# Attention units with scores in one run over four PSUM banks, values in one run, and the side tasks split and spread

## The chip, the cores and the metric

The program runs on one core of one Trainium2 chip. The metric is the device time of one execution in microseconds; the kernel before took 880.97 us (median of three runs, 880.14 to 883.23). The profiled execution, from which all rows below come, took 881.46 us.

## What is computed

Two stages. The first is sliding-window attention with a linear bias by head; its output, one row of 512 numbers for each of 4,608 tokens, goes into the second, a mixture of eight experts in which each token is sent to one expert only.

```python
scores = scale * np.matmul(q, k.transpose(0, 1, 3, 2))       # q, k, v: (8, 8, 576, 64), float32
mask = (rel >= 0) & (rel < 128)
scores = np.where(mask, scores + bias[None], -1000000000.0)  # bias = -slope(head) * distance
attn = softmax(scores); x = np.matmul(attn, v)               # -> (4608, 512)
expert_idx = np.argmax(x @ w_gate, axis=1)                   # 8 experts
h = np.maximum(x_sorted[lo:hi] @ w1[e], 0.0)                 # 512 -> 1024
y_sorted[lo:hi] = h @ w2[e]                                  # 1024 -> 512
out = gate_w[:, None] * y
```

## The kernel before, in words

**Units.** The attention stage is cut into `NU` = 32 units: one for each of 8 batches and of 4 pairs of heads (`b, hp = divmod(u, HP)`). Each unit has, for its two heads (`par` 0 and 1, which lie in the two halves of the partitions):

- `scores`: transposed scores for five blocks of keys (`BLK`: 256, 256, 256, 192 and 64 queries), 10 matrix products per head pair, each two instructions on TensorE. A head has 1,024 score columns, that is two PSUM banks of 512 (`s` = 0 and 1), so a unit needs four banks `sp`. ScalarE takes the exponential of each bank into `e`, VectorE multiplies by a table of exp(bias) and mask into `probs` (`fac` for half 0, `fac2` for half 1).
- `merge` (GpSimd): two additions that fold overlapping blocks of `probs` into `mg`, so that the sums of the softmax cost fewer columns.
- `values`: `probs` times `v` for two stretches of queries (`SEG`, `s` = 0: 256 and `s` = 1: 320), each into a PSUM bank `xp`, which ScalarE copies to `xT`.
- `totals`: products with a column of ones that add up the sums of `probs` and `mg` in a bank `sm`; after a batch's fourth unit it is copied to `sT`.

The work of one unit is recorded beside that of the unit before: in step `u` TensorE gets the scores of unit `u` and the values and totals of unit `u - 1`. Before the change the order in a step is scores half 0, values half 0, scores half 1, values half 1, totals.

**Tasks.** When a batch is complete, a list of tasks is queued (`tasks_of`), which turn it into rows for the experts: two of `logits_t` (products with the gate's weights into a bank `m`, ScalarE copies to `lT`), `gate` (transposes of `lT` and `sT` in banks `m`; VectorE divides, reduces, picks the expert with `pick`; ScalarE has one small exponential `gex` per tile of 128 tokens), `row` (four transposes of `xT` into a bank `m`, VectorE scales them into `xs`, GpSimd writes the token's number), `place` (two small products on what `pick` left in `pre`, VectorE makes `slots`), and `send` (GpSimd scatters a tile's rows to `x_rows` in DRAM by an indirect DMA, line 174). An even batch has 4 tiles, an odd one 5. From step 8 on, 3 or 4 tasks are taken from the list at the end of each step; what is left after the last unit runs in a row.

**Order and buffers.** `tc.manual_schedule()` keeps the order of the code on every engine, so an instruction that waits holds up what stands behind it on its engine. The eight PSUM banks are: three for `sp`, two for `xp`, two for `m`, one for `sm`. Tiles of a pool rotate: a new one waits until the tile that had its bank has been read. `ex` has two buffers of each of `e`, `probs` and `mg`.

**Loads.** SyncE issues, in the code's order, the loads of a batch's q, k and v one batch ahead (two buffers), and in steps 1 to 8 `clear_rows`, eight writes of 1,285 KB that clear `x_rows` in DRAM; the first `send` waits for the last of them.

After the attention come the experts (`gather` reads `x_rows` back; `layer1`, `layer2`), which the change does not touch. Lines from 504 on stand a few lines lower after the change.

Of the kernel before, what the change touches and what calls it, by code (L numbers as in the profile page):

```python
# [8 lines left out]
F32 = mybir.dt.float32  # L9
I32 = mybir.dt.int32  # L10
AX = mybir.AxisListType.X
AF = mybir.ActivationFunctionType
# [9 lines left out]
def kernel(  # L22
# [320 lines left out]
    with tc.tile_pool(name="tab", bufs=1) as tab, \  # L343
# [4 lines left out]
         tc.tile_pool(name="ps_s", bufs=3, space=PSUM) as ps_s, \  # L348
         tc.tile_pool(name="ps_x", bufs=2, space=PSUM) as ps_x, \
         tc.tile_pool(name="ps_1", bufs=1, space=PSUM) as ps_1, \  # L350
         tc.tile_pool(name="ps_m", bufs=2, space=PSUM) as ps_m:
# [37 lines left out]
        probs, xps, mgs, sums = {}, {}, {}, {}  # L389
# [16 lines left out]
        def scores(u, s):  # L406
            b, hp = divmod(u, HP)
            if s == 0:
                probs[u] = ex.tile([P, 2, W], F32, name="probs")
            blocks = [x for x in BLK if x[1] // (W // 2) == s]  # L410
            sps = [ps_s.tile([P, W // 2], F32, name="sp") for _ in range(2)]
            for j, c, q0, n in blocks:
                c -= s * (W // 2)
                for par in range(2):
                    half = slice(par * HALF, (par + 1) * HALF)
                    nc.tensor.matmul(  # L416
                        sps[par][:, c : c + n], lhsT=k_sb[b][half, hp, k_lo[j] : k_lo[j] + P],
                        rhs=q_sb[b][half, hp, q0 : q0 + n], start=True, stop=True,
                    )
            e = ex.tile([P, 2, W // 2], F32, name="e")  # L420
            for par in range(2):
                nc.scalar.activation(e[:, par, :], sps[par][:], AF.Exp, scale=D ** -0.5)  # L422
# [20 lines left out]
        def values(u, s):  # L443
# [5 lines left out]
            xp = ps_x.tile([P, S - 2 * P], F32, name="xp")  # L449
# [53 lines left out]
        def gate(ts):  # L503
            t0, n = ts[0], len(ts)
            tt = slice(t0, t0 + n)
            lgw = rows.tile([P, GT, H, E], F32, name="lgw", bufs=1)
            for i0 in range(0, n, 2):
                two = range(i0, min(i0 + 2, n))
                m = ps_m.tile([P, 2, 3 * HALF], F32, name="m")
                for i in two:  # L510
                    pair, c = ts[i] // TP, ts[i] % TP * P
                    nc.tensor.transpose(m[:, i - i0, :P], lT[pair][:, c : c + P], ident[:])
                    nc.tensor.transpose(m[:, i - i0, P:], sT[pair][:, c : c + P], ident[:64, :64])
                nc.vector.reciprocal(
                    rs_all[:, t0 + i0 : t0 + i0 + len(two), :].rearrange("p t (g a) -> p t g a", a=2),
                    m[:, : len(two), P:].rearrange("p t (a g) -> p t g a", a=2)[:, :, :HP, :],
                )
                for i in two:
                    nc.vector.tensor_tensor(
                        lgw[:, i].rearrange("p (g a) e -> p g a e", a=2),  # L520
                        m[:, i - i0, :P].rearrange("p (g r) -> p g r", r=32)[:, :, : 2 * E]
                        .rearrange("p g (a e) -> p g a e", a=2),
                        rs_all[:, ts[i], :].rearrange("p (g a) -> p g a", a=2).unsqueeze(3).to_broadcast([P, HP, 2, E]),
                        op=ALU.mult,
                    )
# [10 lines left out]
        xs_of = {}  # L536
# [24 lines left out]
        def tasks_of(b):  # L561
            t0 = b // 2 * TP + b % 2 * KT
            tiles = list(range(t0, t0 + KT + b % 2))
            ts = [lambda: logits_t(b, 0), lambda: logits_t(b, 1)]
            ts += [lambda: gate(tiles), lambda: row(tiles, 0), lambda: place(tiles, rows, ps_m, "m"), lambda: row(tiles, 1)]
            for i in range(2, len(tiles)):
                ts.append(lambda i=i: (send(tiles, i - 2), row(tiles, i)))
            return ts + [lambda i=i: send(tiles, i) for i in (len(tiles) - 2, len(tiles) - 1)]

        with tc.manual_schedule():  # L570
# [3 lines left out]
            tasks = []  # L574
            for u in range(NU + 1):
                b, hp = divmod(u, HP)
                if u < NU:
# [6 lines left out]
                    scores(u, 0)  # L584
                if u > 0:
                    values(u - 1, 0)
                if u < NU:
                    scores(u, 1)
                    merge(u)
                if u > 0:  # L590
# [263 lines left out]
```

## Time and profile before

| | us |
|---|---|
| median of 3 runs | 880.97 |
| profiled execution | 881.46 |
| its span, first to last instruction | 879.70 |
| start to the scores of unit 2 | 20.91 |
| units 2 to 7, no tasks | 29.43 |
| units 8 to 31, with tasks | 191.36 |
| last values, last batch's tasks, gather | 24.94 |
| experts | 613.06 |

The five stretches are cut where TensorE starts the scores of unit 2 and of unit 8, the values of unit 31, and the first transposes of the experts. A row of the timeline gives start, duration, engine, line, operation, tiles out<-in, and in brackets how long the engine was idle before it and what ended that. Neighbours of one group on one engine are merged (x8: eight instructions). TensorE's matmuls overlap, so that starts, not durations, tell how long a group holds the engine.

### The profile page before, as it was taken

The page shows a single profiled execution, that of the slowest core. Times are in us where ns is not written, and L with a number is a line of the kernel's source. Part 1 is how long each engine was busy: PE and PEld are TensorE (multiplying, and loading weights), DVE is VectorE, ACT ScalarE, POOL GpSimd, SP SyncE. Part 2 cuts the span into 40 slices and gives each one's busy share as a digit, 9 for nine tenths or more (in the row PEclk, how much of TensorE's full clock was granted, in tenths as well). Part 3 has the DMA queues.
Part 4 walks back from the last instruction along what each step waited for, and adds up shares of the span by engine and source line. Part 5 has one row for each costly group of instructions (what it writes and reads, how often), then busy time and mean ns, then how long its engine had stood idle before and what let it go on. Part 6 is the DMA issues. An engine that isn't in the chain of part 4 may idle for free.

```text
span 879.7 us, 10068 instructions
## 1 busy us (share of the span) xinstructions
PE 827.6 (94%) x4162; PEld 516.8 (59%) x4162; DVE 222.2 (25%) x475; ACT 176.4 (20%) x410; POOL 176.7 (20%) x189
## 2 busy tenths in 40 slices
PE   6998988999958999999999999999999999999993
PEld 4765666666636745754754664674575575475471
DVE  4556556656673100110110120120011011010010
ACT  3653443554410101010100101000100010101010
POOL 5645444566430001001001001001000100100100
PEclk9998898999968999999999999999999999999997
DMA  9997761561125203301600700600420240050060
GB/s 347 347 357 257 262 216 65 214 216 38 37 97 209 102 25 135 144 16 58 235 12 37 258 1 36 251 11 32 164 114 25 83 187 12 37 212 13 36 219 4
DMA packets 47334, 112.54 MB, mean 128 GB/s; under 512 B 3503, under 2 KB 3503, under 8 KB 47280
## 3 DMA queue, kind: packets, MB, share of 16 engines
q1 hardware_dynamic: 40512, 92.89, 30.0%
q0 software_dynamic: 6240, 18.92, 5.7%
q8 instruction: 34, 0.56, 0.3%
q14 instruction: 20, 0.16, 0.1%
q10 hardware_dynamic: 528, 0.02, 0.0%
HBM read 82.37 MB, written 31.01 MB: 129 GB/s over the span
## 4 chain that ended last, share of the span: by engine, by line
issue 64%; POOL 5%; POOLq 0%; DMA 0%
POOL out_dram L751 5%; POOLq L751 0%; DMA x_rows<-xs,slots 0%; POOLq L801 0%
## 5 line engine op out<-in xcount | busy, mean ns | idle before, releaser
L745 PE MATMUL zp<-w,h_sb 128*128 128x512 f32 x672 | 292.4, 592 | 0.0
L732 PE MATMUL hps<-xgT,w 128*128 128x320 f32 (+1 forms) x1152 | 291.8, 415 | 0.0
L732 PEld LDWEIGHTS hps<-xgT,w 128*128 128x128 f32 x1152 | 209.0, 190 | 83.9 <-issue 4.3
L745 PEld LDWEIGHTS zp<-w,h_sb 128*128 128x128 f32 x672 | 125.8, 190 | 149.2 <-issue 149.2
L751 POOL DMA_INDIRECT out_dram<-zo,si x42 | 40.7, 970 | 567.0 <-ACT zo L750 567.0
L737 DVE TENSOR_SCALAR h_sb<-hps 128x320 f32<-128x320 f32 (+1 forms) x72 | 33.8, 469 | 461.6 <-PE hps L732 461.6
L416 PE MATMUL sp<-q_sb,k_sb 64*128 64x256 f32 (+2 forms) x640 | 87.4, 392 | 10.0 <-DMA k_sb<-in_kT_dram 6.3
L422 ACT ACTIVATE e<-sp 128x512 f32<-128x512 f32 x128 | 69.3, 593 | 87.1 <-PE sp L416 83.9
L739 ACT ACTIVATE h_sb<-hps 128x320 f32<-128x320 f32 (+1 forms) x72 | 30.2, 420 | 277.1 <-PE hps L732 277.1
L750 ACT ACTIVATE zo<-zp,xg 128x512 f32<-128x512 f32 x42 | 28.9, 687 | 279.0 <-PE zp L745 279.0
L416 PEld LDWEIGHTS sp<-q_sb,k_sb 64*128 64x128 f32 x640 | 62.9, 204 | 28.9 <-ACT e L422 12.4
L438 POOL TENSOR_TENSOR mg<-probs 128x768 f32<-128x768 f32 x31 | 57.1, 1843 | 101.6 <-PE m L550 47.9
L457 PE MATMUL xp<-probs,v_sb 128*64 128x256 f32 (+3 forms) x768 | 73.7, 330 | 1.9 <-DVE probs L426 1.9
L457 PEld LDWEIGHTS xp<-probs,v_sb 128*64 128x64 f32 x768 | 49.2, 142 | 28.2 <-issue 11.6
L426 DVE TENSOR_TENSOR probs<-e,fac 128x1024 f32<-128x1024 f32 x32 | 40.8, 1273 | 52.1 <-ACT e L422 47.8
L174 POOL DMA_INDIRECT x_rows<-xs,slots x36 | 43.4, 1206 | 19.9 <-DVE cnt L171 9.4
L431 DVE TENSOR_TENSOR probs<-e,fac 128x1024 f32<-128x1024 f32 x32 | 39.5, 1234 | 22.4 <-ACT e L422 22.4
L723 DVE COPY xgT<-tp 128x512 f32<-128x512 f32 x42 | 27.7, 687 | 45.0 <-PE tp L722 45.0
L722 PE MATMUL tp<-ident,xg 128*128 128x128 f32 x168 | 24.7, 290 | 10.3 <-DMA xg<-x_rows 10.2
L722 PEld LDWEIGHTS tp<-ident,xg 128*128 128x128 f32 x168 | 21.4, 150 | 20.5 <-issue 13.6
L550 PE MATMUL m<-ident,xT 128*128 128x128 f32 x144 | 23.4, 300 | 6.2 <-DVE xs L553 5.3
L464 ACT COPY xT<-xp 128x256 f32<-128x256 f32 x64 | 25.6, 400 | 13.4 <-PE xp L457 7.7
(127 smaller groups left out, 291.2 us busy)
## 6 DMA issues: line engine op xcount, KB each, us to landing
w<-in_moe_w_dram SPq DMA_DIRECT2D x20, 2048.0 KB, 17.7
x_rows<-zero_row SPq DMA_DIRECT2D x8, 1285.0 KB
v_sb<-in_v_dram SPq DMA_DIRECT2D x8, 1024.0 KB
q_sb<-in_qT_dram SPq DMA_DIRECT2D x7, 1152.0 KB
k_sb<-in_kT_dram SPq DMA_DIRECT2D x7, 1152.0 KB, 16.6
xg<-x_rows SPq DMA_DIRECT2D x8, 771.0 KB, 5.4
xg<-x_rows SPq DMA_DIRECT2D x8, 514.0 KB
v_sb<-in_v_dram SPq DMA_DIRECT2D x8, 256.0 KB, 7.8
```

The lines of the kernel that those rows point to most:

```text
L174: ins = nc.gpsimd.indirect_dma_start(out=x_d[:, :], out_offset=bass.IndirectOffsetOnAxis(ap=slots[:, t : t + 1], axis=0), in_=row, in_offs ...
L416: nc.tensor.matmul(sps[par][:, c : c + n], lhsT=k_sb[b][half, hp, k_lo[j] : k_lo[j] + P], rhs=q_sb[b][half, hp, q0 : q0 + n], start=True, ...
L422: nc.scalar.activation(e[:, par, :], sps[par][:], AF.Exp, scale=D ** -0.5)
L426: nc.vector.tensor_tensor(to.rearrange("p a (j c) -> p a j c", c=2 * P), e.rearrange("p a (j c) -> p a j c", c=2 * P), fac[:, heads, None, ...
L431: nc.vector.tensor_tensor(to, e[:], fac2[:, heads, :], op=ALU.mult)
L438: eng.tensor_add(mg[:, :, : 3 * P].rearrange("p a (t c) -> p a t c", c=P), two[:, :, :, 0, :], two[:, :, :, 1, :],)
L457: nc.tensor.matmul(xp[par * HALF : (par + 1) * HALF, lo - q0 : hi - q0], lhsT=v_sb[b][:, j, h * D : (h + 1) * D], rhs=probs[u][:, par, c + ...
L722: nc.tensor.transpose(tp[:, db, :], g["xg"][:, j, db * P : (db + 1) * P], ident[:])
L732: nc.tensor.matmul(hps[:, :step], lhsT=g["w"][0][:, db, fb * P : (fb + 1) * P], rhs=g["xT"][:, db, c : c + step], start=(db == 0), stop=(d ...
L737: nc.vector.tensor_relu(g["h"][:, fb, c : c + step], hps[:, :step])
L745: nc.tensor.matmul(zp[:], lhsT=g["h"][:, fb, j * P : (j + 1) * P], rhs=g["w"][1][:, fb, :], start=(fb == 0), stop=(fb == FB - 1),)
L751: ins = nc.gpsimd.indirect_dma_start(out=out[:, :], out_offset=bass.IndirectOffsetOnAxis(ap=g["si"][:, j : j + 1], axis=0), in_=zo[:], in_ ...
```

## The change

Scores of a unit are issued in one run into four banks `sp`, then the four exponentials; the multiplications by the tables get a function of their own, `factors(u, s)`. Values of the unit before follow in one run. The banks are four for `sp`, three for `m`, which `values` now shares with the tasks (`xp` has no pool of its own), one for `sm`. `gate` becomes a task for each two tiles, with like transposes side by side. The last two `send`s are one task. Tasks start in step 6; in each step one is taken between `factors(u, 0)` and `factors(u, 1)`, ahead of the values, and two at the end.

```diff
-         tc.tile_pool(name="ps_s", bufs=3, space=PSUM) as ps_s, \
-         tc.tile_pool(name="ps_x", bufs=2, space=PSUM) as ps_x, \
+         tc.tile_pool(name="ps_s", bufs=4, space=PSUM) as ps_s, \
          tc.tile_pool(name="ps_1", bufs=1, space=PSUM) as ps_1, \
-         tc.tile_pool(name="ps_m", bufs=2, space=PSUM) as ps_m:
+         tc.tile_pool(name="ps_m", bufs=3, space=PSUM) as ps_m:
...
+        def scores(u):
             b, hp = divmod(u, HP)
+            probs[u] = ex.tile([P, 2, W], F32, name="probs")
+            sps = [[ps_s.tile([P, W // 2], F32, name="sp") for _ in range(2)] for _ in range(2)]
+            for j, c, q0, n in BLK:
+                s, c = divmod(c, W // 2)
...
+            exps[u] = [ex.tile([P, 2, W // 2], F32, name="e") for _ in range(2)]
+            for s in range(2):
+                for par in range(2):
+                    nc.scalar.activation(exps[u][s][:, par, :], sps[s][par][:], AF.Exp, scale=D ** -0.5)
+
+        def factors(u, s):
+            hp, e = u % HP, exps[u][s]
...
-            xp = ps_x.tile([P, S - 2 * P], F32, name="xp")
+            xp = ps_m.tile([P, S - 2 * P], F32, name="m")
...
-        def gate(ts):
+        def gate(ts, i0):
...
+            two = range(i0, min(i0 + 2, n))
+            m = ps_m.tile([P, 2, 3 * HALF], F32, name="m")
+            for i in two:
+                pair, c = ts[i] // TP, ts[i] % TP * P
+                nc.tensor.transpose(m[:, i - i0, :P], lT[pair][:, c : c + P], ident[:])
+            for i in two:
+                pair, c = ts[i] // TP, ts[i] % TP * P
+                nc.tensor.transpose(m[:, i - i0, P:], sT[pair][:, c : c + P], ident[:64, :64])
...
+            if two[-1] < n - 1:
+                return
...
-            ts += [lambda: gate(tiles), lambda: row(tiles, 0), lambda: place(tiles, rows, ps_m, "m"), lambda: row(tiles, 1)]
+            ts += [lambda i=i: gate(tiles, i) for i in range(0, len(tiles), 2)]
+            ts += [lambda: row(tiles, 0), lambda: place(tiles, rows, ps_m, "m"), lambda: row(tiles, 1)]
             for i in range(2, len(tiles)):
                 ts.append(lambda i=i: (send(tiles, i - 2), row(tiles, i)))
-            return ts + [lambda i=i: send(tiles, i) for i in (len(tiles) - 2, len(tiles) - 1)]
+            return ts + [lambda: [send(tiles, i) for i in (len(tiles) - 2, len(tiles) - 1)]]
...
+                slow = u < 6
...
-                    scores(u, 0)
+                    scores(u)
+                    factors(u, 0)
+                do(0 if slow else 1)
+                if u < NU:
+                    factors(u, 1)
+                    merge(u)
                 if u > 0:
                     values(u - 1, 0)
-                if u < NU:
-                    scores(u, 1)
-                    merge(u)
-                if u > 0:
                     values(u - 1, 1)
                     totals(u - 1)
                     if hp == 0:
                         tasks += tasks_of(b - 1)
-
-                n = 0 if u < E else 3 if len(tasks) < 12 else 4
-                for _ in range(n if u < NU else len(tasks)):
-                    if tasks:
-                        tasks.pop(0)()
+                do(len(tasks) if u == NU else 0 if slow else 2)
```

Three places show how instructions move. The first is TensorE's row of one step without tasks (`sp` scores, `xp` values). Before:

```order
43 L416 MATMUL sp<-q_sb,k_sb 128x256 x4
44 L457 MATMUL xp<-probs,v_sb 64x256 x2
45 L457 MATMUL xp<-probs,v_sb 64x128 x2
46 L416 MATMUL sp<-q_sb,k_sb 128x256 x2
47 L416 MATMUL sp<-q_sb,k_sb 128x192 x2
48 L416 MATMUL sp<-q_sb,k_sb 128x64 x2
49 L457 MATMUL xp<-probs,v_sb 64x128 x2
50 L457 MATMUL xp<-probs,v_sb 64x256 x2
```

The same step after the change, where the values write a bank `m`:

```order
48 L413 MATMUL sp<-q_sb,k_sb 128x256 x6
49 L413 MATMUL sp<-q_sb,k_sb 128x192 x2
50 L413 MATMUL sp<-q_sb,k_sb 128x64 x2
51 L458 MATMUL m<-probs,v_sb 64x256 x2
52 L458 MATMUL m<-probs,v_sb 64x128 x4
53 L458 MATMUL m<-probs,v_sb 64x256 x2
```

Scores and values changed places three times in a step, and now once. The second place is TensorE at the gate of batch 2, a batch of four tiles, before (end of step 14: gate, row 0, place, then the next scores):

```order
222 L512 MATMUL m<-ident,lT 128x128
223 L513 MATMUL m<-ident,sT 128x64
224 L512 MATMUL m<-ident,lT 128x128
225 L513 MATMUL m<-ident,sT 128x64
226 L550 MATMUL m<-ident,xT 128x128 x4
227 L159 MATMUL m<-pre,ones_sq 128x48
228 L160 MATMUL m<-sel_106,lt_strict 128x8x5
229 L416 MATMUL sp<-q_sb,k_sb 128x256 x4
```

And after (last two tiles' gate and row 0 at the end of step 14, place in the middle of step 15):

```order
187 L514 MATMUL m<-ident,lT 128x128 x2
188 L517 MATMUL m<-ident,sT 128x64 x2
189 L556 MATMUL m<-ident,xT 128x128 x4
190 L413 MATMUL sp<-q_sb,k_sb 128x256 x6
191 L413 MATMUL sp<-q_sb,k_sb 128x192 x2
192 L413 MATMUL sp<-q_sb,k_sb 128x64 x2
193 L159 MATMUL m<-pre,ones_sq 128x48
194 L160 MATMUL m<-sel_106,lt_strict 128x8x5
195 L458 MATMUL m<-probs,v_sb 64x256 x2
```

A whole run of scores now stands between gate and place, and like transposes stand together. The third place is GpSimd around the first scatters (`x_rows`), before, where rows 51 and 52 are the merge of unit 9:

```order
51 L438 TENSOR_TENSOR mg<-probs 128x2x384
52 L441 TENSOR_TENSOR mg<-probs 128x2x64
53 L174 DMA x_rows<-xs,slots 36864x514
54 L544 COPY xs<-tok_i 128x2
55 L174 DMA x_rows<-xs,slots 36864x514
56 L438 TENSOR_TENSOR mg<-probs 128x2x384
```

And after, where rows 49 and 50 are the merge of unit 8 and row 54 begins that of unit 9:

```order
49 L439 TENSOR_TENSOR mg<-probs 128x2x384
50 L442 TENSOR_TENSOR mg<-probs 128x2x64
51 L174 DMA x_rows<-xs,slots 36864x514
52 L550 COPY xs<-tok_i 128x2
53 L174 DMA x_rows<-xs,slots 36864x514 x3
54 L439 TENSOR_TENSOR mg<-probs 128x2x384
```

The first scatter now follows the merge of unit 8 instead of 9, and four scatters, not two, stand ahead of the next merge.

## Rows read from the trace of the kernel before

**Rows 1.** Windows: length, busy us of PE, PEld, DVE, ACT, POOL, clock, DMA share, GB/s.

```profile
20.91:50.34 29.43, 29.43 (x338) 21.24 (x336) 14.88 (x13) 17.96 (x38) 18.29 (x12) 1.00 1.05 359
50.34:241.70 191.36, 173.58 (x1673) 122.75 (x1671) 115.15 (x232) 87.98 (x232) 98.83 (x94) 0.94 0.52 178
```

**Rows 2.** Timeline of PE, a step without tasks, up to the next step.

```profile
25.82 1.14 PE L416 MATMUL sp<-q_sb,k_sb 64*128 64x256 f32 x8
26.88 0.87 PE L457 MATMUL xp<-probs,v_sb 128*64 128x256 f32 x8
27.68 1.20 PE L416 MATMUL sp<-q_sb,k_sb 64*128 64x256 f32 x12
28.81 1.31 PE L457 MATMUL xp<-probs,v_sb 128*64 128x128 f32 x16
30.05 0.30 PE L476 MATMUL sm<-probs,one_c 128*32 128x128 f32 x2
30.72 1.13 PE L416 MATMUL sp<-q_sb,k_sb 64*128 64x256 f32 x8
```

**Rows 3.** Timeline of PE, unit 31's values, which no scores divide.

```profile
241.70 1.96 PE L457 MATMUL xp<-probs,v_sb 128*64 128x256 f32 x24
```

**Rows 4.** Waits of PE, 50.34 to 241.70: us in total, times, longest.

```profile
PE m L159 <- DVE gsum L545: 6.5, 3, 2.3
PE m L550 <- DVE xs L553: 5.3, 9, 1.4
PE sp L416 <- ACT e L422: 3.7, 4, 1.3
```

**Rows 5.** Timeline of PE at batch 1's gate and place; eight transposes of rows.

```profile
79.37 0.33 PE L512 MATMUL m<-ident,lT 128*128 128x128 f32 x1
...
79.84 0.33 PE L512 MATMUL m<-ident,lT 128*128 128x128 f32 x1
...
84.90 0.63 PE L159 MATMUL m<-pre,ones_sq 128*128 128x48 f32 x2 [2.16 <-DVE gsum L545]
...
176.36 1.09 PE L550 MATMUL m<-ident,xT 128*128 128x128 f32 x8
```

**Rows 6.** The same gate on DVE and ACT.

```profile
82.54 0.72 DVE L526 TENSOR_REDUCE lgn<-lgw 128x40 f32<-128x320 f32 x1
83.53 0.30 ACT L530 ACTIVATE gex<-lgn,lmin 128x8 f32<-128x8 f32 x1 [4.29 <-DVE lmin L527]
84.88 0.19 ACT L530 ACTIVATION_READ_ACCUMULATOR gex<-lgn,lmin 128x1 f32 x1
```

**Rows 7.** Windows behind that wait; columns as in rows 1.

```profile
84.00:87.00 3.00, 2.10 (x10) 1.88 (x12) 1.99 (x9) 1.06 (x8) 0.00 (x0) 0.50 1.02 407
87.00:90.00 3.00, 3.00 (x18) 1.55 (x16) 0.83 (x1) 1.46 (x3) 0.00 (x0) 0.50 0.11 39
```

**Rows 8.** Timeline of ACT and DVE in the step of rows 2.

```profile
26.98 1.09 ACT L422 ACTIVATE e<-sp 128x512 f32<-128x512 f32 x2 [1.30 <-PE sp L416]
30.16 0.43 ACT L464 COPY xT<-xp 128x320 f32<-128x320 f32 x1 [0.17 <-PE xp L457]
28.15 1.26 DVE L426 TENSOR_TENSOR probs<-e,fac 128x1024 f32<-128x1024 f32 x1 [1.81 <-ACT e L422]
```

**Rows 9.** Groups by form, 50.34 to 241.70: busy us, mean ns, idle before.

```profile
L553 DVE TENSOR_TENSOR xs<-m,rs_all 128x512 f32<-128x512 f32 x31 | 20.4, 678 | 2.5 <-PE m L550 2.4
```

**Rows 10.** Timeline of DVE (unit 1) and POOL: merges of units 0 and 1, first scatter.

```profile
16.89 1.22 DVE L426 TENSOR_TENSOR probs<-e,fac 128x1024 f32<-128x1024 f32 x1
17.05 2.73 POOL L438 TENSOR_TENSOR mg<-probs 128x768 f32<-128x768 f32 x1 [6.28 <-DVE probs L431]
21.36 1.81 POOL L438 TENSOR_TENSOR mg<-probs 128x768 f32<-128x768 f32 x1 [1.17 <-DVE probs L431]
23.13 0.46 POOL L441 TENSOR_TENSOR mg<-probs 128x128 f32<-128x128 f32 x1
71.15 2.06 POOL L174 DMA_INDIRECT x_rows<-xs,slots  x1 [3.42 <-issue]
```

More of the change, by code (lines that the diff above doesn't have):

```diff
@@ L388 @@
         q_sb, k_sb, v_sb, xT, lT, sT = {}, {}, {}, {}, {}, {}
-        probs, xps, mgs, sums = {}, {}, {}, {}
+        probs, exps, mgs, sums = {}, {}, {}, {}
         def load(b):
@@ L404, in load @@
                     nc.sync.dma_start(v_sb[b][:, KT, :], v[(b + 1) * S - P : (b + 1) * S, :])
-        def scores(u, s):
+        def scores(u):
             b, hp = divmod(u, HP)
[L408 to L413, printed above, removed]
+            probs[u] = ex.tile([P, 2, W], F32, name="probs")
+            sps = [[ps_s.tile([P, W // 2], F32, name="sp") for _ in range(2)] for _ in range(2)]
+            for j, c, q0, n in BLK:
+                s, c = divmod(c, W // 2)
                 for par in range(2):
@@ L416, in scores @@
                     nc.tensor.matmul(
-                        sps[par][:, c : c + n], lhsT=k_sb[b][half, hp, k_lo[j] : k_lo[j] + P],
+                        sps[s][par][:, c : c + n], lhsT=k_sb[b][half, hp, k_lo[j] : k_lo[j] + P],
                         rhs=q_sb[b][half, hp, q0 : q0 + n], start=True, stop=True,
                     )
-            e = ex.tile([P, 2, W // 2], F32, name="e")
-            for par in range(2):
-                nc.scalar.activation(e[:, par, :], sps[par][:], AF.Exp, scale=D ** -0.5)
+            exps[u] = [ex.tile([P, 2, W // 2], F32, name="e") for _ in range(2)]
[4 more added lines that the diff above has]
+            hp, e = u % HP, exps[u][s]
             to = probs[u][:, :, s * (W // 2) : (s + 1) * (W // 2)]
@@ L501, in logits_t @@
             nc.scalar.copy(lT[pair][:, o : o + n], lp[:, :n])
-        def gate(ts):
+        def gate(ts, i0):
             t0, n = ts[0], len(ts)
             tt = slice(t0, t0 + n)
[L506 to L516, printed above, removed]
-                )
[L518 to L525, printed above, removed]
@@ new lines, in gate @@
+            if i0 == 0:
+                lgws[t0] = rows.tile([P, GT, H, E], F32, name="lgw", bufs=1)
+            lgw = lgws[t0]
+            two = range(i0, min(i0 + 2, n))
[6 more added lines that the diff above has]
+                nc.tensor.transpose(m[:, i - i0, P:], sT[pair][:, c : c + P], ident[:64, :64])
@@ new lines, in gate @@
+            nc.vector.reciprocal(
+                rs_all[:, t0 + i0 : t0 + i0 + len(two), :].rearrange("p t (g a) -> p t g a", a=2),
+                m[:, : len(two), P:].rearrange("p t (a g) -> p t g a", a=2)[:, :, :HP, :],
+            )
+            for i in two:
+                nc.vector.tensor_tensor(
+                    lgw[:, i].rearrange("p (g a) e -> p g a e", a=2),
+                    m[:, i - i0, :P].rearrange("p (g r) -> p g r", r=32)[:, :, : 2 * E]
+                    .rearrange("p g (a e) -> p g a e", a=2),
+                    rs_all[:, ts[i], :].rearrange("p (g a) -> p g a", a=2).unsqueeze(3).to_broadcast([P, HP, 2, E]),
+                    op=ALU.mult,
+                )
@@ L535 @@
         RG = 2
-        xs_of = {}
+        xs_of, lgws = {}, {}
         def row(ts, i):
@@ L574, with do @@
             tasks = []
+            def do(n):
+                for task in tasks[:n]:
+                    task()
+                del tasks[:n]
             for u in range(NU + 1):
                 b, hp = divmod(u, HP)
+                slow = u < 6
                 if u < NU:
```

## The prediction

> **What bounds the kernel now.** I read the windows first, cut by what TensorE does, and then TensorE's waits and timeline. The change reaches only the attention stage. The experts, 613 of 880 us, run the same program on the same data and only start sooner. In units 2 to 7 TensorE is busy for all of 29.43 us [rows 1], 4.90 us a step (30.72 - 25.82) [rows 2]: nothing is waited for, so what shortens it there is a shorter run of TensorE itself. In steps 8 to 31 it is busy for 173.58 of 191.36 us [rows 1]; the other 17.8 us are waits, nearly all of them for the tasks: 6.5 for `place`, which waits three times for the gate's chain on VectorE, 5.3 for rows that wait for a bank `m`, 3.7 for a score bank whose exponential stands behind `gex` on ScalarE [rows 4]. The granted clock there is 0.94 [rows 1], so about 0.06 x 191.36 = 11.5 us more are lost at the lower of its two levels (1.2 for 2.4 GHz). That level follows long waits: after the 2.16 us before batch 1's `place` [rows 5] the clock was 0.50 for 6 us [rows 7], which costs 3 us. SyncE, VectorE (115 us), ScalarE (88 us) and GpSimd (99 us of 191) [rows 1] have room on the mean, so TensorE's runs and its waits set the stage's time.
>
> **The change, part by part**, against the profiled execution's own 881.46 us (the median of the runs is 880.97, so the two can be taken as one).
>
> *Scores and values in one run each.* A step loses one switch from values to scores and one from scores to values. Values in two runs take 0.80 (27.68 - 26.88) and 1.24 (30.05 - 28.81) [rows 2]. In one run they last 1.96 [rows 3]; a run's record reaches 0.07 past the next start (1.31 for 1.24), so 1.89 against 2.04: 0.15 saved. Scores in one run stand in no row. Half 0, eight instructions, holds the engine for 1.06, half 1, twelve with fewer columns each, for 1.13 [rows 2]; at the pace of half 1 (0.094 each) half 0 would take 0.75, so the saving lies between 0 and 0.31, and I take 0.20, near the other switch. Together 0.35, in 30 steps (units 2 to 31): **-10.5** (-4.5 to -14). Nothing hides this saving, since TensorE is the bound; it could be lost where the next wait is for another engine, which is counted below.
>
> *Like transposes side by side.* A tile's pair of transposes takes 0.47 (79.84 - 79.37), so two tiles 0.94; like transposes follow at 0.13 (1.09 / 8) [rows 5]. Four like that, and one switch pair of 0.47 - 0.26 = 0.21 in place of two, make 0.73. 14 pairs of tiles up to step 31: **-2.9**. In the last batch two pairs stand on the path to the gather: **-0.4**.
>
> *A task in the middle of a step* puts a third kind of work between scores and values: one switch more, 0.15 as above, in the 22 steps whose middle task uses TensorE: **+3.3** (0 to 4.6).
>
> *Old waits go:* **-17.8**.
>
> *New waits.* I lay a step out by hand, from the start of its scores. By the row of the step without tasks the first two exponentials start 1.16 after the scores (26.98 - 25.82), two take 1.09, and VectorE's first multiplication starts 0.08 after them and takes 1.26 [rows 2, 8]. With the change ScalarE then has its four exponentials from 1.2 to 3.4, VectorE multiplies from 2.35 to 3.6, does the middle task's share, and multiplies again for 1.25. TensorE ends scores at 2.0, the middle task at 2.7, values at 4.6, totals at 5.3 (0.67 each, 30.72 - 30.05 [rows 2]), two tasks at 6.4. The three banks rotate, so the first end task takes the middle task's bank: needed at 5.3, free at about 4.3 when VectorE has scaled a row (0.68 [rows 9]). A plain step therefore waits for nothing, with a margin of 1 us. The values find the banks of the tasks before long free, and four score banks are free since 3.4. Exceptions are the steps around a batch's last gate, whose chain takes 2.4 on VectorE (82.54 to the `place` at 84.90 [rows 5, 6]) and whose five `gex` take 1.5 on ScalarE (83.53 to 85.07 [rows 6]), less by some 0.3 each for four tiles:
> - Last gate at a step's end, row 0 in the middle of the next, `place` behind it (batches 1, 4 and 5): the last transposes end at 6.5 (time of the gate's step), VectorE reduces from 7.25, `gex` runs from 8.25 to 9.8 and holds up the exponentials of the next unit, VectorE multiplies from 11.0 to 12.25 and scales row 0 until 13.3; `place` needs that row's bank at 11.7. Wait 1.65, 1.15 with four tiles: 4.45 in all.
> - Last gate in the middle, row 0 and `place` at the end (batches 0 and 3): `place` takes the first values' bank, whose copy stands behind `gex` on ScalarE: 0.95 and 1.45, in all 2.4.
> - Gate and row 0 at the end, `place` in the next middle (batches 2 and 6): 0.35 each, 0.7 in all.
>
> *The first scatters.* The first one waits for the cleared rows; before, it started 3.42 us after GpSimd was free, at 71.15, then took 2.06 [rows 10]. It now stands behind the merge of unit 8, which by the same layout ends near 60, and four scatters stand ahead of the merge of unit 9, which totals need near 70. If the delay is 3.42 again, the merge starts at 60.6 + 3.4 + 2.1 + some 4 for the rest = 70 and ends 2.2 later (1.81 and 0.46 [rows 10]): a wait of about 2.5. If nothing holds the scatter, none; if it can't start before 71 as before, 9. I take 2.5, since the delay is the row there is.
>
> New waits together 7.55 + 2.5: **+10.1** (3 to 20).
>
> *Clock.* Of 11.5 lost before, I expect one fall behind the scatters and one or two behind the waits of 1.45 to 1.65, at 3 us each [rows 7]: 7.5 stay, **-4.0** (0 to -11.5).
>
> *Start.* Unit 0's merge took 2.73 beside a multiplication of VectorE, unit 1's first addition 1.81 [rows 10]. Now both multiplications of unit 1 lie beside it: **+1.0** (0 to 2). In steps 2 to 5, 4.55 us long, the time from the second multiplication to the totals that need the merge stays as it was, since a step's length and the place of the totals shrink together.
>
> Sum: -10.5 - 2.9 - 0.4 + 3.3 - 17.8 + 10.1 - 4.0 + 1.0 = -21.2, so **860 us** (881.46 - 21.2 = 860.3).
>
> **The rivals.**
>
> *The waits only change their name.* The three shared banks and ScalarE's queue around the gate give back all 17.8 us and the clock's 11.5. For it: there is still one gate per batch with the same chain. Against it: `place` no longer follows the gate directly, and score banks no longer run out. Then only the runs, transposes, switches and the start count: -10.5 - 2.9 - 0.4 + 3.3 + 1.0 = -9.5, **872 us**.
>
> *No wait is left*, since the chains are shorter than I lay them out, and the clock stays at its higher level: -9.5 - 17.8 - 11.5, **843 us**. For it: units 2 to 7 show such a stage; against it: ScalarE and VectorE keep their order.
>
> *TensorE idles a little in every step, and the clock falls.* Values had two banks of their own and share three now. If VectorE is more than 1 us later than my layout, every end task waits for the middle task's bank. The place is the first end task of steps 8 to 31, which without waits and at the full clock hold 191.36 - 17.8 - 11.5 - 24 x 0.35 - 2.9 + 3.3 = 154 us. At a mean clock of 0.75, half of it at the level of [rows 7], these take 154 / 0.75 = 205, 51 more: 843 + 51 = **894 us**. It decides below a mean clock of 0.80 (154 / 0.80 - 154 = 39). Against it: 17.8 us of waits in 24 steps left the mean clock at 0.94 [rows 1], and the layout has a margin. The Trainium skill has a rule that speaks for this rival (TensorE: Matmul & The Clock Gate, "A second HAM failure mode: psum-queue depth-cycling"): a kernel that cycles through PSUM banks in each iteration lets TensorE idle briefly between groups of matmuls, and its clock goes back and forth between the levels. By that rule the time would be this rival's. The trace bears it out only behind waits as long as that of rows 5.
>
> **Chances.** The forecast 0.60, waits with new names 0.20, no wait left 0.15, idling banks 0.05. The forecast alone spans 851 to 868 (switches and new waits at a third of their bounds). The range reaches from 843 to 873, which leaves out the last rival and the outer edges of the two before it. What a measurement of this kernel can tell from no change is 0.3%, 2.6 us: faster 0.91, the same 0.04, slower 0.05.
>
> **What would show it.** In the profile after, a step without tasks should take 4.5 to 4.6 us, with 20 score instructions in one group; TensorE's idle time from unit 8 on should be near 10 us, in single waits of 1 to 2 us for VectorE's rows, the copies of values and, once, GpSimd's merge of unit 9; the experts should take 613 us again. A wrong prediction would show as a step of 4.9 us (the switch costs nothing), as idle time of about 18 us or about 0, or as a clock below 0.9 in the stage.

## The result, and the profile after

The changed kernel takes **856.21 us** (median of 4 runs, 854.81 to 857.57) where the kernel before takes 880.57 (4 runs, 880.14 to 883.23): a ratio of 0.9717, with a 95% interval of 0.9691 to 0.9744. The profiled execution took 855.47 us, 26.0 less than that of before, with a span of 853.7. By the same cuts as in the table of before:

| stretch | before, us | after, us |
|---|---|---|
| start to the scores of unit 2 | 20.91 | 22.26 |
| units 2 to 7 | 29.43 | 33.56 (two of the steps now have tasks) |
| units 8 to 31 | 191.36 | 161.38 |
| last values, last tasks, gather | 24.94 | 23.36 |
| experts | 613.06 | 613.1 |

A step without tasks, from the timeline of TensorE, to set beside [rows 2]:

```profile
28.83 2.06 PE L413 MATMUL sp<-q_sb,k_sb 64*128 64x256 f32 x20
30.82 1.96 PE L458 MATMUL m<-probs,v_sb 128*64 128x256 f32 x24
32.71 0.30 PE L477 MATMUL sm<-probs,one_c 128*32 128x128 f32 x2
...
33.39 0.92 PE L413 MATMUL sp<-q_sb,k_sb 64*128 64x256 f32 x6
```

Twenty scores hold the engine for 1.99 us (30.82 - 28.83) in place of 2.19, values for 1.89 in place of 2.04, and the step takes 4.56 in place of 4.90. What TensorE waits for from 50.3 to 217.2 us, in total, number and longest, beside [rows 4]:

```profile
PE sm L477 <- POOL mg L442: 9.3, 3, 6.3
PE m L159 <- ACT xT L465: 2.3, 3, 1.2
PE m L159 <- DVE gsum L551: 0.7, 1, 0.7
PE m L159 <- ACT gex L536: 0.3, 1, 0.3
PE m L556 <- DVE xs L559: 0.3, 1, 0.3
...
```

The old list is nearly gone: `place` (L159) waits 3.3 us in place of 6.5, rows 0.3 in place of 5.3, scores not at all. A new line stands on top: totals that wait for GpSimd's merge. The windows (length, busy time of each engine, granted clock, DMA share, GB/s):

```profile
20.00:25.00 5.00, 3.96 (x22) 2.43 (x24) 0.68 (x1) 0.64 (x2) 3.17 (x3) 0.50 1.07 394
50.30:217.20 166.90, 153.40 (x1693) 117.92 (x1690) 121.49 (x230) 87.51 (x236) 97.97 (x95) 0.98 0.59 204
78.00:81.00 3.00, 2.22 (x12) 0.78 (x12) 0.00 (x0) 0.00 (x0) 3.00 (x5) 0.50 0.00 0
```

From 50.3 us, so that the first wait of a task (in step 7) is taken in, to the values of unit 31 TensorE is idle for 13.5 us (166.9 - 153.4), in place of 17.8. The clock is 0.98 in place of 0.94: one fall, at 78 to 84 us, at the end of the wait of 6.3. GpSimd's timeline shows where that wait comes from:

```profile
61.37 1.81 POOL L439 TENSOR_TENSOR mg<-probs 128x768 f32<-128x768 f32 x1 [1.86 <-DVE gsum L551]
...
70.68 1.45 POOL L174 DMA_INDIRECT x_rows<-xs,slots  x1 [7.09 <-issue]
...
75.52 0.97 POOL L174 DMA_INDIRECT x_rows<-xs,slots  x1 [0.30 <-issue]
76.50 1.82 POOL L439 TENSOR_TENSOR mg<-probs 128x768 f32<-128x768 f32 x1
78.26 0.47 POOL L442 TENSOR_TENSOR mg<-probs 128x128 f32<-128x128 f32 x1
```

GpSimd stands for 7.09 us ahead of the first scatter, then four scatters stand ahead of the merge of unit 9, which TensorE has needed since 72.4. The start, on TensorE:

```profile
21.05 1.28 PE L477 MATMUL sm<-mg,one_c 128*32 128x320 f32 x8 [1.65 <-POOL mg L442]
22.26 3.89 PE L413 MATMUL sp<-q_sb,k_sb 64*128 64x256 f32 x20
```

Totals of unit 0 wait 1.65 us for a merge that lies beside VectorE's multiplications (2.72 and 1.43 us for its two additions, 1.81 and 0.45 later), and unit 2's scores take 3.89 us at the lower clock, where unit 3's take 2.06.

### The profile page after: what moved, and what is told of

Read it like the earlier page. It is cut to its first block, busy times and chain, and to the rows that moved or that the text cites. A ratio compares the mean times of both kernels' runs of the same rounds, so it can differ in the third digit from the quotient of the medians.

```text
span 853.7 us, 10090 instructions
## 1 busy us (share of the span) xinstructions
PE 802.2 (94%) x4162; PEld 511.6 (60%) x4162; DVE 227.8 (27%) x475; ACT 173.9 (20%) x410; POOL 171.5 (20%) x189
## 4 chain that ended last, share of the span: by engine, by line
issue 69%; PE 15%; POOL 9%; DVE 5%; ACT 1%; POOLq 0%; DVEq 0%
PE sp L413 5%; POOL out_dram L763 5%; PE m L458 4%; PE sm L477 2%; PE m L556 2%; POOL x_rows L174 1%; POOL mg L439 1%; DVE probs L427 1%; PE m L498 1%; POOL mg L442 1%; DVE probs L432 1%; ACT gex L536 1%; DVE lgn L532 1%; PE m L514 1%; DVE xs L559 0%
## 5 line engine op out<-in xcount | busy, mean ns | idle before, releaser
L751 ACT ACTIVATE h_sb<-hps 128x320 f32<-128x320 f32 (+1 forms) x72 | 30.2, 419 | 277.1 <-PE hps L744 277.1
L413 PE MATMUL sp<-q_sb,k_sb 64*128 64x256 f32 (+2 forms) x640 | 71.5, 368 | 6.4 <-DMA k_sb<-in_kT_dram 6.4
L420 ACT ACTIVATE e<-sp 128x512 f32<-128x512 f32 x128 | 66.2, 599 | 48.1 <-PE sp L413 44.8
L413 PEld LDWEIGHTS sp<-q_sb,k_sb 64*128 64x128 f32 x640 | 63.0, 199 | 17.8 <-issue 11.1
L458 PE MATMUL m<-probs,v_sb 128*64 128x256 f32 (+3 forms) x768 | 64.2, 316 | 3.7 <-DVE probs L427 2.8
L458 PEld LDWEIGHTS m<-probs,v_sb 128*64 128x64 f32 x768 | 48.4, 138 | 19.9 <-DVE probs L427 2.9
L427 DVE TENSOR_TENSOR probs<-e,fac 128x1024 f32<-128x1024 f32 x32 | 43.6, 1361 | 43.8 <-ACT e L420 34.1
L174 POOL DMA_INDIRECT x_rows<-xs,slots x36 | 39.8, 1104 | 22.8 <-issue 12.0
L432 DVE TENSOR_TENSOR probs<-e,fac 128x1024 f32<-128x1024 f32 x32 | 41.9, 1309 | 0.7 <-ACT e L420 0.5
L477 PE MATMUL sm<-mg,one_c 128*32 128x320 f32 (+1 forms) x256 | 24.5, 373 | 11.0 <-POOL mg L442 11.0
L734 PE MATMUL tp<-ident,xg 128*128 128x128 f32 x168 | 24.6, 289 | 10.6 <-DMA xg<-x_rows 10.5
L465 ACT COPY xT<-m 128x256 f32<-128x256 f32 x64 | 25.3, 402 | 22.9 <-PE m L458 22.9
## 6 DMA issues: line engine op xcount, KB each, us to landing
k_sb<-in_kT_dram SPq DMA_DIRECT2D x7, 1152.0 KB, 11.5
```

The source lines that it names most:

```text
L174: ins = nc.gpsimd.indirect_dma_start(out=x_d[:, :], out_offset=bass.IndirectOffsetOnAxis(ap=slots[:, t : t + 1], axis=0), in_=row, in_offs ...
L413: nc.tensor.matmul(sps[s][par][:, c : c + n], lhsT=k_sb[b][half, hp, k_lo[j] : k_lo[j] + P], rhs=q_sb[b][half, hp, q0 : q0 + n], start=Tru ...
L420: nc.scalar.activation(exps[u][s][:, par, :], sps[s][par][:], AF.Exp, scale=D ** -0.5)
L427: nc.vector.tensor_tensor(to.rearrange("p a (j c) -> p a j c", c=2 * P), e.rearrange("p a (j c) -> p a j c", c=2 * P), fac[:, heads, None, ...
L458: nc.tensor.matmul(xp[par * HALF : (par + 1) * HALF, lo - q0 : hi - q0], lhsT=v_sb[b][:, j, h * D : (h + 1) * D], rhs=probs[u][:, par, c + ...
L477: nc.tensor.matmul(sm[g : g + 32, c : c + n], lhsT=one_c[:, hp, :], rhs=src[:, par, s0 : s0 + n], start=(hp == 0 and c == 0), stop=(hp == ...
```

## Experiments: which part brings what

**The runs alone.** Kernel before, with the new `scores`, `factors`, `values` and banks; `gate` and tasks as before. Against the kernel after, without the lines of `gate`:

```diff
-            ts += [lambda i=i: gate(tiles, i) for i in range(0, len(tiles), 2)]
-            ts += [lambda: row(tiles, 0), lambda: place(tiles, rows, ps_m, "m"), lambda: row(tiles, 1)]
+            ts += [lambda: gate(tiles), lambda: row(tiles, 0), lambda: place(tiles, rows, ps_m, "m"), lambda: row(tiles, 1)]
...
-                slow = u < 6
+                slow = u < E
...
-                do(0 if slow else 1)
...
-                do(len(tasks) if u == NU else 0 if slow else 2)
+                do(len(tasks) if u == NU else 0 if slow else 3 if len(tasks) < 12 else 4)
```

> The kernel before with the scores of a unit in one run over four banks, the values in one run, and the three shared banks; the tasks, the gate and their places stay as before. My theory (each part of the change is worth its own term): a step without tasks takes 4.55 us, 30 steps save 10.5 us, the start costs 3 us (GpSimd's merge of unit 0, as in the kernel after), and most of the 17.8 us of old waits and the lower clock stay, since the gate with place right behind it stays: 871 to 876 us. Rival A, the runs in one carry the whole gain since they also take away the waits for score banks and with them the clock's falls: 856 to 862 us. Rival B, three banks shared by values and by tasks in a row of three or four make the values wait: idle time over 20 us and 876 us or more.

862.56 us (ratio 0.9780, 0.9758 to 0.9802), 19.2 less than before: rival A's size, and not mine. The waits of TensorE from 45 to 222 us, and a window over nearly all of the stage with tasks:

```profile
PE m L159 <- DVE gsum L546: 7.5, 3, 2.8
PE sm L477 <- POOL mg L442: 4.0, 3, 1.4
...
```

```profile
55.50:222.18 166.68, 153.13 (x1632) 118.65 (x1629) 115.24 (x231) 82.76 (x227) 94.30 (x92) 0.97 0.56 191
```

`place` still waits, as I said. But the 3.7 us of scores and the 5.3 of rows [rows 4] are gone although no task was moved. So the runs and their banks bring more than shorter runs. TensorE is idle for 13.6 us here (166.68 - 153.13) and for 13.5 in the whole change: beside the runs, the spread tasks buy no idle time. They take waits from `place` (7.5 and, not shown, 0.4 us here, 3.3 there) and give them to the late merges (4.0 here, 9.3 there). The 6.4 us by which the whole change is faster lie for the most part in the transposes (4.1), in the clock (0.97 here, 0.98 there) and behind the last unit's scores (25.1 us from the values of unit 31 to the experts here, 23.4 there).

**The tasks alone.** Kernel before with the new `gate`, `tasks_of` and `do`; scores, values and banks in their old form. Against the kernel before, the last part:

```diff
                     scores(u, 1)
+                do(0 if u < 6 else 1)
+                if u < NU:
                     merge(u)
...
-                n = 0 if u < E else 3 if len(tasks) < 12 else 4
-                for _ in range(n if u < NU else len(tasks)):
-                    if tasks:
-                        tasks.pop(0)()
+                do(len(tasks) if u == NU else 0 if u < 6 else 2)
```

> The kernel before with the split gate, its like transposes side by side and one task in the middle of a step (behind the second half of the scores) and two at its end from unit 6 on; scores and values stay in two halves with the banks as before. My theory: the transposes give 4.3 us, the spreading of tasks some 4 us of waits and 6 to 8 us of clock, so 864 to 868 us, with a step without tasks of 4.90 us and the merge of unit 9 late behind the first scatters as in the kernel after (a wait of 4 to 6 us). Rival A, the spreading alone brings nothing since values and tasks find only two task banks and three score banks: 875 us or more, TensorE idle for 17 us or more in steps 6 to 31. Rival B, nearly all of the gain is here: 858 us or less.

870.76 us (0.9870, 0.9849 to 0.9891), 11.0 less than before; between my 864 to 868 and rival A. Waits from 45 to 232 us:

```profile
PE m L159 <- DVE gsum L550: 5.4, 2, 2.8
PE sm L476 <- POOL mg L441: 4.6, 1, 4.6
PE sp L416 <- ACT e L422: 3.5, 4, 1.6
...
```

Spreading takes away the rows' 5.3 us too (0.4 is left), but not the scores' wait with three score banks. 19.2 and 11.0 make 30.2, the whole change 24.4: the two parts take away some of the same waits, and each brings late merges.

**The runs alone, with two shared banks.** The kernel of the runs alone with `bufs=2` for `ps_m`.

> The kernel with the runs alone (scores and values each in one run, tasks as before) and two shared banks in place of three. It asks what took away the 5.3 us that rows waited for banks before, and the 3.7 us of scores behind the exponentials, when only the runs and banks were changed. Theory: the third shared bank took away the first and the fourth score bank the second; with two banks the rows wait again, 5 us or more in all, and the time is 867 to 875 us, while no score waits for an exponential. Rival: the order of the runs did it, since values now come late in a step: 862 to 865 us and no wait of rows over 1 us in all.

868.22 us (0.9863, 0.9843 to 0.9883), 5.7 more than with three. The first lines of its waits, 45 to 220 us:

```profile
PE m L551 <- DVE xs L554: 6.6, 9, 1.7
PE m L159 <- DVE gsum L546: 5.9, 3, 2.3
PE m L551 <- ACT xT L465: 2.3, 3, 1.0
```

As expected: the rows wait again, nine times for VectorE, and no score does. So with the runs it is the third shared bank that takes away the rows' waits. The scores' waits are gone in both kernels with the runs over four score banks, and are there in the tasks alone, which has neither (3.5 us). Whether the fourth bank or the order does it isn't shown, since no run parts the two.

**The change with two shared banks.**

```diff
-         tc.tile_pool(name="ps_m", bufs=3, space=PSUM) as ps_m:
+         tc.tile_pool(name="ps_m", bufs=2, space=PSUM) as ps_m:
```

> The kernel after with two shared banks for values and tasks in place of three. It tests the margin of 1 us a step that the prediction's layout gave the third bank, and the rival by which a little idle time in every step brings the clock down. Theory: the second values of a step now take the middle task's bank, which VectorE frees 0.8 us too late by the layout, in some 19 steps with a row, a gate or logits in the middle: 10 to 18 us of waits in pieces of about 0.8 us and the clock stays near 1: 866 to 875 us. Rival A, short idle times in every step bring the clock back and forth: a mean clock below 0.85 from unit 8 on and 885 us or more. Rival B, the third bank does nothing: 855 to 858 us.

872.69 us (0.9908, 0.9891 to 0.9924), 16.5 more than after. Of its waits from 45 to 223 us three of the four largest, and a window that holds most of the short ones:

```profile
PE m L458 <- DVE xs L559: 6.6, 7, 1.1
PE m L458 <- DVE lgw L523: 6.1, 6, 1.5
...
PE m L458 <- ACT xT L465: 4.5, 3, 2.2
```

```profile
85.00:220.00 135.00, 118.11 (x1292) 89.55 (x1292) 83.36 (x167) 65.14 (x170) 76.88 (x74) 0.99 0.54 186
```

Values now wait for a shared bank to be read, 16 times in these lines, for rows 0.94 us on the mean (6.6 / 7) where the layout gave 0.8. From 85 to 220 us TensorE is idle for 16.9 of 135 us, in some sixteen pieces of 2.2 us at most, and the clock is 0.99. So the margin was the right quantity, and rival A, the prediction's last rival, falls: this idling in short pieces left the clock high. The Trainium skill's rule (TensorE: Matmul & The Clock Gate, "A second HAM failure mode: psum-queue depth-cycling"), which the page tells of a bf16 kernel, is not borne out by this float32 one.

**No task in the middle.**

```diff
-                do(0 if slow else 1)
-                do(len(tasks) if u == NU else 0 if slow else 2)
+                do(len(tasks) if u == NU else 0 if slow else 3)
```

> The kernel after with all three tasks at the end of a step and none in its middle. Theory: 22 switches between scores and values go, which the trace after prices at 1.2 us in all (the prediction said 3.3), but in some batches the last gate, row 0 and place then stand in one row, so place waits 2 to 2.5 us there as in the run with the runs alone: 857 to 862 us. Rival: the middle task brings nothing but its switches: 852 to 855 us.

858.49 us (0.9753, 0.9734 to 0.9772), 2.3 more than after, less than the two intervals can tell apart. Its waits show both sides: `place` waits 7.7 us in three places, some 2.6 each, and totals wait 3.3 us for merges in place of 9.3. The middle place is worth little in sum.

**Transposes in pairs.**

```diff
                 nc.tensor.transpose(m[:, i - i0, :P], lT[pair][:, c : c + P], ident[:])
-            for i in two:
-                pair, c = ts[i] // TP, ts[i] % TP * P
```

> The kernel after with the transposes of two tiles one pair after the other, as before, in place of like beside like. Theory by the rows of the two traces: two tiles take 0.633 us side by side and 0.93 in pairs, so 14 pairs of tiles up to the last unit cost 4.1 us and two behind it 0.6: 860 to 862 us. By the term of the prediction (0.21 a pair) it would be 859 to 860 us. Rival: the gate's transposes stand where TensorE would wait anyway, and nothing is lost: 855 to 857 us.

859.59 us (0.9758, 0.9742 to 0.9774), 3.4 more. In its timeline two tiles take 0.92 us (225.26 - 224.34); side by side they took 0.63 (221.40 - 220.77 in the trace after), so 0.29 a pair of tiles and not 0.21. Sixteen pairs at 0.29 would make 4.6 us, at 0.21 3.4: the time alone can't tell the two, and the row decides. Most of it isn't hidden by other work.

## Experiments: the late merges and the start

**First tasks one unit later.** `slow = u < 7`.

> The kernel after with its first tasks one unit later (unit 7 in place of 6), so that the four first scatters stand ahead of the merge of unit 10 and not of unit 9. Theory: the first scatter can't start before about 70 us whatever is done, the four of them then end near 76, and the merge of unit 10, which is needed near 78, ends near 78.5. The wait of 6.3 us shrinks to 1 us or less and the half clock behind it (3.4 us) goes: 846 to 850 us. Rival: the work of batch 0 is only pushed back, a task is left over for the time after the last unit and other merges are late in place of this one: 854 to 858 us.

851.92 us (0.9665, 0.9643 to 0.9686), 4.3 less than after and 2 above the expected 846 to 850; the wait falls from 6.34 to 2.90 us. It is no smaller since totals need the merge of unit 10 at 74.6, earlier than I had laid out, and it ran from 74.2 to 77.4. The clock falls behind it all the same (0.50 from 78 to 84 us). The waits in steps 25 and 29 (for the merges of units 24 and 28) fall from 2.98 to 0.64, and `place` waits 1.5 us more.

**Loads of batch 3 one unit later.**

```diff
-                    if hp == 1 and 1 < b + 1 < NB:
+                    if hp == (2 if b == 2 else 1) and 1 < b + 1 < NB:
```

> The kernel after with the loads of batch 3 issued one unit later (unit 10 in place of 9), so that the DMA queues are nearly empty from about 62 to 67 us. Theory: the first scatter has everything it waits for at 65.0 us and then stands 5.5 us because GpSimd's next block of instructions is fetched through DMA queues that the loads fill (the fetch runs at 68.7 us). With the queues empty it starts before 67.5 us, the wait of totals for the merge of unit 9 falls from 6.3 to 3 us or less, and the time is 850 to 853 us, if batch 3's loads still come before unit 12. Rival, the first scatter takes some 5 us to start wherever it stands: it starts at 70 to 71 us as before and the time is 855 to 858 us, or more by a wait of unit 12 for its loads.

856.90 us (0.9723, 0.9693 to 0.9754): the edit does not do what it was meant to. Nothing else stands between the two places on SyncE, so the order of every engine's instructions is the same and the loads start when they did. It is a second measurement of the changed kernel, and says that 70.68 and 70.38 us for the first scatter are one value.

**A scatter to a spare array early on GpSimd.** (The array's line is left out.)

```diff
+                    if u == 2:
+                        nc.gpsimd.indirect_dma_start(
+                            out=spare[:, :], out_offset=bass.IndirectOffsetOnAxis(ap=tok_i[:, 0:1], axis=0),
+                            in_=zero_row[:], in_offset=None, bounds_check=P - 1, oob_is_err=False,
+                        )
```

> The kernel after with one more scatter, of rows of zeros to a spare array that nobody reads, on GpSimd between the merges of units 1 and 2. In all six kernels so far the first scatter starts 1.7 us after a fetch of instructions of 8 KB has run on the DMA queues (68.97 and 70.68 us in the kernel after), though all that it waits for was there at 65.0. Theory: the fetch is tied to the first use of this kind of instruction and is slow in coming beside the loads; used once early, where GpSimd is idle from 23.2 to 28.7 us, it is there already, and the first real scatter starts at 65 to 66 us: the wait of totals for the merge of unit 9 falls from 6.3 to 2 us or less and the time to 847 to 851 us. Rival: the fetch is tied to the place in the instruction stream and not to the kind: the first real scatter starts at 69 to 72 us again and the time is 855 to 858 us.

852.12 us (0.9680, 0.9664 to 0.9696), 4.1 less, a little above the expected 847 to 851. GpSimd:

```profile
23.52 1.17 POOL L602 DMA_INDIRECT spare_rows<-zero_row,tok_i  x1 [0.18 <-issue]
62.38 0.45 POOL L444 TENSOR_TENSOR mg<-probs 128x128 f32<-128x128 f32 x1
66.27 0.99 POOL L176 DMA_INDIRECT x_rows<-xs,slots  x1 [3.43 <-issue]
```

The first real scatter starts 4.4 us earlier and the wait falls to 2.80 us. But the reason that I gave for it falls: the spare scatter, the first of its kind, started 0.18 us after the merge with no fetch at all. The fetch came at 64.32 to 64.63, in the time in which GpSimd waits for the cleared rows anyway, where in the kernel after it came at 68.67, after that wait had ended at 64.98. That fits a fetch that belongs to a place in the instruction stream, as the rival has it, with this place moved by the added instructions; the rival's times (69 to 72, 855 us or more) did not come.

**Merge ahead of the middle task's scatters.** `send` keeps a middle task's scatters back until `merge(u)` is issued.

> The kernel after with the scatters of a middle task issued behind the unit's merge on GpSimd and not ahead of it. Theory: of the 9.3 us that totals wait for merges, the two waits of 1.2 and 1.8 us at units 25 and 29 go, since three or four scatters stood ahead of those merges, and the one of 6.3 us becomes about 4 (two scatters stand ahead of the merge in place of four); the clock falls behind it all the same. 850 to 852 us. Rival: the scatters behind the merge make the next merge late, or a row waits for its buffer: 855 us or more.

855.12 us (0.9707, 0.9683 to 0.9732): 1.1 less than after, which can't be told from no change. The wait for unit 9's merge fell to 3.80 as expected and that of step 29 went, but in step 25 one of 2.78 stands in place of 1.21: four scatters, one of them kept back, now run there ahead of the next merge, where three did. There, and in the time, the rival was right.

**Merge of unit 0 on VectorE.**

```diff
-            eng = nc.vector if u == NU - 1 else nc.gpsimd
+            eng = nc.vector if u in (0, NU - 1) else nc.gpsimd
```

> The kernel after with the merge of unit 0 on VectorE in place of GpSimd. Theory: in the kernel after, totals of unit 0 wait 1.65 us for GpSimd's merge, which lies beside both multiplications of unit 1 (2.72 + 1.43 us), and TensorE then runs unit 2 at its lower clock (about 2.1 us lost). On VectorE the merge ends about 18 us, so the wait goes and with it, if the wait is what drops the clock, the lower clock: 852.5 to 854.5 us, scores of unit 2 at 20 to 20.6 us. Rival: the lower clock comes from the earlier waits of the first values for VectorE (2.75 and 0.70 us) and stays, and VectorE's multiplications of unit 1 come later by the merge: 855 to 857 us.

852.09 us (0.9681, 0.9662 to 0.9699), 4.1 less. TensorE at the start:

```profile
18.21 0.73 PE L477 MATMUL sm<-mg,one_c 128*32 128x320 f32 x8
18.87 2.06 PE L413 MATMUL sp<-q_sb,k_sb 64*128 64x256 f32 x20
```

Unit 2's scores start 3.4 us earlier and at the full clock. The 1.65 us of the wait are settled. The share of the clock isn't: from 20 to 25 us it is 0.50 in the kernel after, 0.71 in the second measurement of the same program, and 1.00 in the run with later tasks, whose program is the same up to there. In the kernel after it is 0.63 already from 15 to 20 us, so it fell before the wait for the merge, which begins at 19.4. That the merge lowers the clock is not shown.

**Both.** Merge of unit 0 on VectorE, first tasks at unit 8, and a third task at a step's end while more than eleven are open:

```diff
-                slow = u < 6
+                slow = u < E
-                do(len(tasks) if u == NU else 0 if slow else 2)
+                do(len(tasks) if u == NU else 0 if slow else 3 if len(tasks) > 11 else 2)
```

> The kernel after with the merge of unit 0 on VectorE, the first tasks at unit 8 and a third task at a step's end while over eleven are open. Theory: the 3.4 us of the start are saved as in the run of that edit alone, the first scatters stand ahead of the merge of unit 11, which is needed near 80 us, so the wait of 6.3 us and the 3.4 us lost at the lower clock behind it go; other waits change by 2 us at most: 845 to 848 us. Rival: the tasks pushed back make other merges and places late, or leave work for the time after the last unit: 851 to 854 us, no better than either edit alone.

**843.18 us** (5 runs, 842.11 to 844.64; ratio 0.9574, 0.9558 to 0.9590), 13.0 less than after and below the expected 845 to 848. Its waits from 19 to 204 us and its clock:

```profile
PE m L159 <- DVE gsum L551: 1.7, 2, 0.9
...
PE sm L477 <- POOL mg L442: 1.0, 2, 0.7
```

```profile
24.00:212.00 188.00, 179.63 (x2028) 136.70 (x2018) 141.00 (x259) 102.81 (x274) 115.00 (x107) 1.00 0.68 235
```

The late merges cost 1.0 us in place of 9.3, and the attention keeps the full clock. Three edits went in together; what the third task at a step's end is worth by itself was not measured.

## Why the prediction came out right

The forecast of 860 us (-21.2) stands against -26.0 in the profiled executions; the direction, the place and the main mechanism (shorter runs, fewer waits, a higher clock) were right, and several terms were mis-sized in ways that partly cancel.

| step of the prediction | forecast | measured | where |
|---|---|---|---|
| scores and values in one run | -10.5 | -10.5 | 0.20 and 0.15 a step, 30 steps |
| like transposes | -2.9 | -4.1 | 0.29 for each of 14 pairs |
| a task in the middle | +3.3 | +1.2 | starts on TensorE, below |
| old waits less new waits | -7.7 | -4.3 | 17.8 to 13.5 idle |
| clock in the stage | -4.0 | -8.2 | 11.5 lost to 3.3 |
| start | +1.0 | +3.4 | 1.35 later, 2.0 at the lower clock |
| tail | -0.4 | -1.6 | 24.94 to 23.36 |

The measured column adds up to -24.1; 1.9 of the 26.0 I can't assign. That the sum came so near is in part luck: the waits came out 3.4 us worse and the start 2.4, while the clock was 4.2 better, the middle task 2.1, the transposes and the tail 1.2 each.

- *Runs.* The switch of scores was taken "near the other switch", a guess between bounds of 0 and 0.31, and is 0.20.
- *Middle task.* I priced each of 22 switches at 0.15. A row in the middle costs 0.58 and one of two at the end 0.51:

```profile
211.03 1.09 PE L556 MATMUL m<-ident,xT 128*128 128x128 f32 x8
212.06 2.06 PE L413 MATMUL sp<-q_sb,k_sb 64*128 64x256 f32 x20
214.05 0.66 PE L556 MATMUL m<-ident,xT 128*128 128x128 f32 x4
214.63 1.96 PE L458 MATMUL m<-probs,v_sb 128*64 128x256 f32 x24
```

  Eleven rows at 0.07, three logits at 0.1, two `place` at 0.07, gates at nothing: 1.2.
- *New waits.* The list around the gate (7.55) was laid out too tightly: all that TensorE waits for beside the merges is 4.2. The first scatters were the step that failed: "If the delay is 3.42 again" counted from the moment when GpSimd is free. The scatter doesn't follow GpSimd; in ten of the thirteen other profiles it started between 69.15 and 71.98 us, whether GpSimd was free at 61.9 or at 68.3. That a scatter "can't start before 71 as before" was the outer bound (9) of my term; 6.34 came. The waits in steps 25 (1.21) and 29 (1.77), for merges that stand behind three and four scatters, were not in the list at all.
- *Old waits.* The prediction let all 17.8 us go in one term, without saying to which part. The runs alone show that the runs with their four score banks and the third shared bank end 9.0 of them (3.7 and 5.3) with no task moved.
- *Rivals.* Three quarters of the waits did come back under other names, but in ten pieces in place of 22, one of them long, and the clock came back, which "the waits only change their name" had excluded. The idling banks were settled by the run with two banks.
- *Start.* The merge beside both multiplications came out as laid out (2.72 + 1.43 us), and the delay of 1.35 lies near the 1.0 forecast. The lower clock there (unit 2's step takes 6.57 us in place of 4.56) was in no term; as the runs of the same program above differ in it, it can't be put down to the change.

## What to carry to other kernels

When work is moved to an earlier place, ask for each engine's queue what it is moved ahead of: here four scatters ahead of a merge, the first of them late, cost 6.3 us and a fall of the clock behind it, and beginning the tasks two units later gave 13 us together with one merge on another engine and a third task in the fuller steps. A bank more in a shared rotation can be worth as much as a better order of tasks (the third bank 5.7 us with the old order and 16.5 with the new, the new order 6.4), and the run with one bank less tells its price. Moving an issue in the code means nothing if no other instruction of its queue stands between the two places.

## What the runs showed of the hardware

**GpSimd stood for 5.5 us, in all likelihood for a fetch of instructions.** In thirteen of fourteen profiles the first scatter to `x_rows` starts 1.64 to 1.72 us after the end of one fetch on the instruction queue q14. In the kernel after the fetch runs from 68.67 to 68.97, the scatter's first instruction comes at 70.48 and the scatter at 70.68, and its semaphores were all there at 64.98. The profile doesn't say whose instructions a packet of q14 brings; that they are GpSimd's is read from this constant gap. The DMA totals of that moment (68.6 to 69.0 us):

```profile
q1 hardware_dynamic: 74, 0.15, 97.1%
q14 instruction: 1, 0.01, 4.8%
```

The loads keep the DMA engines full until about 71 us. In the fourteenth profile, with merge 0 on VectorE alone, GpSimd has two instructions fewer, and the scatter starts at 65.66, ahead of the fetch (69.14 to 69.45). The Trainium skill (Runtime: NRT & Kernel Launch, "Instruction fetch mechanics") calls the crossing of a block mostly hidden; here one, if this fetch is such a crossing, was not. That full DMA queues make it late is not shown: with the spare scatter it came at 64.32 through queues as full (403 GB/s from 63 to 67 us), and no run with empty queues was made.

**The clock.** Length of a wait alone doesn't decide. With the first tasks one unit later the clock fell behind a wait of 2.90 us. With the merge ahead of the scatters it stayed behind one of 2.78 us, though TensorE was busy for only 0.26 of 3 us. With merge 0 on VectorE it fell behind a wait of 1.22 us that ended at 172.76. The windows of the one where it stayed, and then of the last:

```profile
175.00:178.00 3.00, 0.26 (x4) 0.00 (x0) 2.68 (x1) 0.39 (x1) 3.00 (x3) 1.00 0.74 261
178.00:181.00 3.00, 2.96 (x27) 2.11 (x28) 1.46 (x6) 0.00 (x0) 2.30 (x3) 1.00 0.01 1
```

```profile
171.00:174.00 3.00, 1.78 (x22) 0.76 (x18) 2.97 (x5) 0.42 (x1) 1.71 (x2) 1.00 0.77 295
174.00:177.00 3.00, 3.00 (x19) 2.83 (x19) 2.69 (x11) 0.78 (x6) 2.35 (x3) 0.63 0.10 35
```

What decides between them stays open.
